# A searched order of work, smaller transfers and paired stores in an attention-and-filter kernel on one core

## The chip, the cores and the metric

The kernel runs on one core of a Trainium2 chip. The metric is the device time of one execution in microseconds (us), lower is better. "Span" is the time from the first to the last instruction in the profiled execution; it is about 1.7 us shorter than the device time of the same execution. Unless a sentence says otherwise, "clock" is the clock that was granted to TensorE, as a share of full speed.

A run is called slow when it is over 1.5% above the fastest run of the same kernel; the others are called fast. Ratios use fast runs alone.

## The reference, cut to what matters

Two branches work on the same x (2048 rows of 640, bf16) and are mixed row by row by a gate. Branch A is attention in four segments of 512 rows, 32 heads of 20, with a memory M, z that is carried from segment to segment. Branch B is a filter: a 2-D FFT, a product with complex weights, and the inverse FFT.

```python
for s in range(4):                                  # branch A, segments of 512 rows
    logits = einsum('bhqd,bhkd->bhqk', qs, ks) * scale + mask
    a_dot  = einsum('bhqk,bhkd->bhqd', softmax(logits), vs)
    pq     = phi(qs)                                # where(t > 0, t + 1, exp(t))
    a_mem  = einsum('bhld,bhde->bhle', pq, M) / (einsum('bhld,bhd->bhl', pq, z)[..., None] + 1e-6)
    outs.append(g * a_mem + (1 - g) * a_dot)        # g = sigmoid(beta), one number a head
    M = M + einsum('bhld,bhle->bhde', phi(ks), vs)
    z = z + phi(ks).sum over rows
a = concat(outs) @ wo
b = irfft2(rfft2(x) * (w_r + 1j * w_i))             # branch B
gate = sigmoid((x * gate_w).sum(-1, keepdims=True))
return gate * a + (1 - gate) * b
```

## The kernel before

The program does not write its instructions in the order in which they are to run. It first records about 2,400 operations. Each has the engines that may do it, its predecessors, an estimated duration and a priority (a time at which it would be wanted). A list scheduler inside the program then simulates the engines, gives each engine the ready operation of lowest priority, and fixes order, engine, PSUM bank and DMA semaphore. The simulation decides only the order: on the chip each engine waits for semaphores, so a wrong duration gives no wrong result, only waits.

In the simulation of the kernel before, a DMA moves 230 bytes a ns and lands 1,900 ns later, every issue takes 450 ns, and a matmul always runs at full clock.

```python
class Sched:
    HOP = 70.0
    DMABW = 230.0
    ...
                fn, occ, lat = o.alts[e]
                busy_until[e] = now + occ
                if o.dma:
                    st = max(bw_free, now + occ)
                    bw_free = st + o.nbytes / self.DMABW
                    ...
                    o.t1 = bw_free + 1900.0
```

The operations that the argument touches are these. `fold` on VectorE and GpSimd prepares x for the FFT (tiles `xf`, `xsb`), and matmuls with `fcat` transform it into `Ac`. `xt_load` brings a segment's x transposed, by a DMA that transposes. `proj_tile` computes one 128-row tile of q or k, evicts it from PSUM to one of three staging tiles `qu`, and stores it to a scratch tensor in HBM. The "pad" loads bring it back with each head's 20 rows at a partition offset of 32, and read 32 rows to do so.

```python
    O_STEP, FIN, V0, XT1 = 7.35, (4.71, 1.77), 3.96, 4.43      # XT1: priority of the second segment's xt_load
    ...
    def proj_tile(self, s, which, t, prio, xT, xb):
        ...
        self.quc = getattr(self, "quc", -1) + 1
        qi = self.quc % 3
        qu, qb = self.qu[qi], b("qu", qi)
        ...
        self.Sc.op(self.copy_alts(lambda: qu.ap(0, [1, L]), lambda: self.ps(bank, 0, [1, L]), L),
                   r=[bank], w=[qb], prio=prio, name="ev_proj")
        scr = self.qd if which == "q" else self.kd
        self.dma(lambda: dap(scr.ap(), s * 656 * L + t * P * L, [L, P], [1, L]), lambda: qu.ap(0, [1, L]),
                 P * L * 2, [qb], [b(which + "d", s, t)], prio, name="st_" + which)
    ...
    # pad loads: for each group of heads j, 32 rows of the scratch tensor to partitions 32 j ...
    dst = pad.ap(g0 * L, [L, 4 - g0], [1, L], p0=32 * j, np_=32)
    src = dap(scr.ap(), s * 656 * L + (320 * half + 80 * g0 + 20 * j) * L, [L, 32], [80 * L, 4 - g0], [1, L])
    ...
    # finish_tile: 128 rows of the output, as 4 x 32 rows
    self.dma(lambda: dap(self.out, (s * L + 4 * a) * D, [D, 4], [16 * D, 32], [1, D]), lambda: ot.ap(0, [1, D]), P * D * 2, otb,
             [b("out", s, a)], prio, name="st_out")
```

In the profile every matmul has one line (a helper), L548 before and L567 after, so matmuls are told apart by their tiles.

The softmax here doesn't subtract the row's maximum and nothing guards it: scores larger than these inputs give would overflow.

## Time and profile before

| kernel before | |
|---|---|
| median of 3 runs | 286.04 us (285.66 to 289.02) |
| profiled run: span, mean clock | 282.7 us, 0.951 |
| TensorE (PE) busy | 252.3 us, 89% |
| VectorE (DVE), ScalarE (ACT), GpSimd (POOL) busy | 201.2, 202.8, 194.6 us |
| end of the last matmul | 276.6 us |
| half-clock windows of 3.413 us before that | 7 |

The last row is from the clock record in the trace: its half-clock stretches last 13.653, 3.413, 3.413 and 3.413 us.

First some lines of the page of the kernel before. PE, DVE and PEclk are rows of 40 equal slices of 7.1 us: busy tenths of TensorE and VectorE, and the granted clock in tenths. The last line shown is the chain of work that ended last, by engine.

```profile
span 282.7 us, 8310 instructions
PE 252.3 (89%) x3356; PEld 144.4 (51%) x3376; DVE 201.2 (71%) x523; ACT 202.8 (72%) x205; POOL 194.6 (69%) x265
...
PE   8997975999889999596999998999899899999991
...
DVE  0379999598699788955899889797978454344410
...
PEclk9999985799799999888999999999999999999997
...
PE 61%; DVE 19%; ACT 5%; DMA 4%; POOL 4%; issue 4%; SPq 1%; DVEq 0%
```

TensorE is the spine. The clock row dips near 40 to 54, 77 and 120 to 136 us, which are the four stretches of the clock record (40.0 to 53.6, 74.1 to 77.5, 118.5 to 121.9 and 132.1 to 135.5 us). Stretches of 10 us show the two places that matter most. The columns are: stretch, length, busy us (and instructions) of PE, its weight loads, DVE, ACT and POOL, then the granted clock, the DMA share and GB/s.

```profile
40.00:50.00 10.00, 6.29 (x75) 3.47 (x75) 9.76 (x22) 7.05 (x7) 8.48 (x9) 0.50 0.83 186
50.00:60.00 10.00, 9.95 (x128) 5.13 (x128) 6.17 (x14) 7.40 (x8) 8.43 (x12) 0.82 0.32 74
...
110.00:120.00 10.00, 6.91 (x74) 4.16 (x73) 9.96 (x32) 7.77 (x8) 8.33 (x13) 0.92 0.75 186
120.00:130.00 10.00, 8.78 (x118) 4.15 (x117) 4.78 (x12) 7.64 (x7) 6.40 (x8) 0.91 0.54 152
130.00:140.00 10.00, 8.48 (x87) 5.10 (x89) 8.15 (x21) 6.63 (x11) 9.25 (x13) 0.83 0.49 129
```

At 40 to 50 us TensorE does 6.29 us of work at half clock while VectorE is full. Busy time at half clock counts half: in the four half-clock stretches TensorE was busy for 18.6 us, so full clock would have saved 9.3 us.

What it waits for stands in the timeline of TensorE in the kernel before (start, duration, what, and in brackets the idle time before it and what ended that):

```profile
43.78 0.61 PE L548 MATMUL psum<-qp_108,kp_110 20*128 20x256 bf16 x8 [1.66 <-ACT ex L1064]
...
49.77 1.91 PE L548 MATMUL psum<-xT_98,wq 128*128 128x512 bf16 x4 [1.07 <-DVE xsb L809]
...
119.06 1.91 PE L548 MATMUL psum<-xT_97,wk 128*128 128x512 bf16 x4 [2.47 <-ACT et_103 L936]
...
130.14 0.99 PE L548 MATMUL psum<-big,Ac 128*128 128x161 bf16 x6 [1.31 <-DVE qu_100 L558]
```

The second line is the first matmul on the second segment's x. The last one waited for VectorE to evict into the staging tile `qu_100`, and VectorE's own timeline says why that was late:

```profile
129.40 0.69 DVE L558 CAST qu_100<-psum 128x512 bf16<-128x512 f32 x1 [3.41 <-DMA k_scr<-qu_100]
```

VectorE sat idle for 3.41 us until the store of the tile's previous contents had landed. That store stood late in the DMA queue of SyncE (SPq: start of an issue and its length):

```profile
115.36 3.10 SPq L575 DMA_TRANSPOSE xT_98<-in_A_x_dram  x1
...
127.35 0.53 SPq L577 DMA_DIRECT2D k_scr<-qu_100  x1
```

The end has no holes to fill. The last pieces of the chain (start, duration, what):

```profile
224.94 34.80 PE psum L548 x542
...
262.12 14.51 PE psum L548 x353
276.65 0.44 ACT ot_87 L556
```

### The profile page before, as it was taken

How to read it: one execution, taken by the hardware profiler on the slowest of the kernel's cores; microseconds unless marked ns; L12 is line 12 of the kernel's file. 1: busy time of each engine (PE TensorE's matmuls, PEld its weight loads, DVE VectorE, ACT ScalarE, POOL GpSimd, SP SyncE). 2: the span in 40 equal slices, each digit the busy share in tenths (PEclk: the TensorE clock that was granted, in tenths of full speed). 3: DMA queues.
4: the chain of work that ended last, by engine and by line, in shares of the span. 5: the costliest groups of instructions: out<-in, count | busy, mean ns of one | idle time of the engine just before them, and what ended most of it. 6: DMA issues, size and time to landing. Idle time of an engine off the chain costs nothing.

```text
span 282.7 us, 8310 instructions
## 1 busy us (share of the span) xinstructions
PE 252.3 (89%) x3356; PEld 144.4 (51%) x3376; DVE 201.2 (71%) x523; ACT 202.8 (72%) x205; POOL 194.6 (69%) x265
## 2 busy tenths in 40 slices
PE   8997975999889999596999998999899899999991
PEld 2432543364547466244555565656465645454590
DVE  0379999598699788955899889797978454344410
ACT  1485477787784878686778897888689877667441
POOL 7059778979866757785989977898778745253410
PEclk9999985799799999888999999999999999999997
DMA  8956999254995675955624766513475403763112
GB/s 183 314 173 180 286 192 205 54 157 122 261 148 118 156 181 141 237 151 143 129 87 127 124 133 217 157 57 112 99 189 156 81 20 78 108 105 84 60 48 73
DMA packets 59270, 39.91 MB, mean 141 GB/s; under 512 B 32168, under 2 KB 55512, under 8 KB 59224
## 3 DMA queue, kind: packets, MB, share of 16 engines
q1 hardware_dynamic: 57920, 38.89, 56.9%
q10 hardware_dynamic: 1312, 0.49, 0.7%
q8 instruction: 26, 0.43, 0.6%
q14 instruction: 12, 0.10, 0.1%
HBM read 22.98 MB, written 9.97 MB: 117 GB/s over the span
## 4 chain that ended last, share of the span: by engine, by line
PE 61%; DVE 19%; ACT 5%; DMA 4%; POOL 4%; issue 4%; SPq 1%; DVEq 0%
PE psum L548 61%; ACT ex L1064 4%; DVE xsb L809 4%; DMA xT_97<-in_A_x_dram 2%; DMA gbc<-g_scr 1%; SPq L577 1%; DVE va_112 L972 1%; POOL ex L1067 1%; DVE Ac L558 1%; DVE Cp L558 1%; DVE et_102 L946 1%; POOL fbg_83 L907 1%; POOL fbg_82 L907 1%; DVE xf_118 L804 1%; DVE Pt_67 L1213 1%
## 5 line engine op out<-in xcount | busy, mean ns | idle before, releaser
L1064 ACT ACTIVATE ex<-psum 128x2048 bf16<-128x2048 f32 x80 | 150.1, 1876 | 27.2 <-PE psum L548 26.4
L1067 POOL TENSOR_SCALAR_AFFINE_SELECT ex<-ex 128x512 bf16<-128x512 bf16 x128 | 80.9, 651 | 43.2 <-ACT ex L1064 40.6
L548 PEld LDWEIGHTS psum<-va_112,ex 128*128 128x128 bf16 x640 | 19.1, 97 | 4.1 <-ACT qu_99 L556 0.8
L548 PEld LDWEIGHTS psum<-va_113,ex 128*128 128x128 bf16 x640 | 18.6, 96 | 5.0 <-issue 1.6
L548 PE MATMUL psum<-va_113,ex 128*128 128x21 bf16 x640 | 20.2, 173 | 1.0 <-POOL ex L1067 0.8
L548 PE MATMUL psum<-va_112,ex 128*128 128x21 bf16 x640 | 20.1, 174 | 0.7 <-ACT qu_99 L556 0.7
L548 PE MATMUL psum<-big,Ac 128*128 128x161 bf16 (+2 forms) x96 | 18.1, 322 | 2.1 <-DVE qu_100 L558 1.3
L548 PE MATMUL psum<-qp_108,kp_110 20*128 20x128 bf16 (+3 forms) x256 | 16.5, 312 | 2.0 <-ACT ex L1064 1.7
L548 PE MATMUL psum<-xT_97,wk 128*128 128x512 bf16 (+1 forms) x86 | 15.2, 391 | 2.7 <-ACT et_103 L936 2.5
L548 PE MATMUL psum<-big,Cp 128*128 128x321 bf16 (+1 forms) x96 | 16.7, 301 | 0.4 <-DVE G L558 0.4
L548 PE MATMUL psum<-qp_109,kp_111 20*128 20x128 bf16 (+3 forms) x256 | 16.3, 307 | 0.8 <-ACT gate_128 L970 0.6
L1106 POOL TENSOR_TENSOR on_116<-on_116,mem 128x320 bf16<-128x320 bf16 x16 | 12.6, 790 | 5.9 <-DVE on_116 L1098 3.4
L1218 POOL TENSOR_TENSOR Yt_68<-Pt_66 128x321 bf16<-128x321 bf16 x16 | 11.9, 750 | 6.6 <-DVE Pt_66 L1213 4.7
L548 PE MATMUL psum<-wv,xT_97 128*128 128x500 bf16 (+1 forms) x80 | 13.8, 307 | 2.8 <-DVE q_9_79 L558 1.5
L1213 DVE TENSOR_TENSOR Pt_67<-psum,Wt_63 128x321 bf16<-128x321 f32 x32 | 14.1, 482 | 2.5 <-PE psum L548 2.5
L548 PE MATMUL psum<-xT_97,wq 128*128 128x512 bf16 (+1 forms) x86 | 15.3, 386 | 0.6 <-DMA xT_97<-in_A_x_dram 0.4
L1213 DVE TENSOR_TENSOR Pt_66<-psum,Wt_62 128x321 bf16<-128x321 f32 x32 | 14.1, 482 | 1.9 <-PE psum L548 1.9
L548 PE MATMUL psum<-xT_98,wq 128*128 128x512 bf16 x44 | 14.0, 442 | 1.6 <-DVE xsb L809 1.1
L548 PE MATMUL psum<-wv,xT_98 128*128 128x500 bf16 (+1 forms) x80 | 14.4, 300 | 0.0
L548 PEld LDWEIGHTS psum<-big,Ac 128*128 128x128 bf16 x96 | 9.6, 113 | 7.6 <-DVE Cp L558 2.1
L1218 POOL TENSOR_TENSOR Yt_69<-Pt_67 128x321 bf16<-128x321 bf16 x16 | 11.7, 739 | 1.9 <-DVE Pt_67 L1213 1.9
L548 PE MATMUL psum<-xT_98,wk 128*128 128x512 bf16 x44 | 12.0, 381 | 0.2
(214 smaller groups left out, 546.7 us busy)
## 6 DMA issues: line engine op xcount, KB each, us to landing
xsb<-in_A_x_dram SPq DMA_DIRECT2D x8, 320.0 KB, 4.6
qp_109<-q_scr SPq DMA_DIRECT2D x16, 128.0 KB, 2.7
kp_111<-k_scr SPq DMA_DIRECT2D x16, 128.0 KB, 3.0
tt_59<-tab_tt SPq DMA_DIRECT2D x6, 256.0 KB, 2.7
qp_108<-q_scr SPq DMA_DIRECT2D x12, 128.0 KB, 4.2
kp_110<-k_scr SPq DMA_DIRECT2D x12, 128.0 KB, 2.7
tt_60<-tab_tt SPq DMA_DIRECT2D x5, 256.0 KB, 3.8
tt_61<-tab_tt SPq DMA_DIRECT2D x5, 256.0 KB, 3.2
```

What stands on the lines that cost most here:

```text
L548: h = e.matmul(o_, l_, r_, start=st, stop=sp_, **kw)
L558: alts["dve"] = (lambda e: e.tensor_copy(dst(), src()), 75 + 1.04 * n, 85.0)
L577: return e.dma_start(d_, s_)
L804: self.either(lambda e, r=r, op=op: e.tensor_tensor(xf.ap(r * 642, [321, 2], [1, 320]), xs.ap(o, [D, 2], [1, 320]), xs.ap(o + 320, [D, 2], ...
L809: self.either(lambda e, dst=dst, src=src, d0=d0, n=n, op=op: e.tensor_tensor(xs.ap(o + dst, [D, 2], [1, n]), xf.ap(src + d0, [321, 2], [1, ...
L907: fn = lambda e: e.tensor_tensor(fb.ap(0, [L, 2], [32, 16], [1, 32]), self.fcat.ap(256 + 32 * s, [P, 2], [0, 16], [1, 32]), self.gbc.ap(0, ...
L946: fmin = lambda e: e.tensor_scalar(et.ap(0, [1, L]), et.ap(0, [1, L]), 1.0, None, ALU.min)
L1064: self.one("act", lambda e: e.activation(dst(), src(), ACT.Exp, scale=SC), 4 * width, [bank], [self.exb(s, g, j) for g, j in outs], prio - ...
L1067: self.one("pool", lambda e, g=g, j=j: e.affine_select(self.ex.ap(self.exo(s, g) + JOFF[j], [1280, 4], [1, P]), self.ex.ap(self.exo(s, g) ...
L1106: add(*args, lambda e, g=g: e.tensor_tensor(on.ap(80 * g, [D, 4], [1, 80]), on.ap(80 * g, [D, 4], [1, 80]), self.mem.ap(80 * g, [D, 4], [1 ...
L1213: self.one("dve", lambda e, r=r, ri=ri, Pt=Pt, Wt=Wt, bank=bank: e.tensor_tensor(Pt.ap((2 * r + ri) * 322, [1, KD]), self.ps(bank, 0, [1, ...
L1218: fn = lambda e, r=r, a0=a0, a1=a1, op=op, Pt=Pt, Yt=Yt: e.tensor_tensor(Yt.ap(r * 322, [1, KD]), Pt.ap(a0 * 322, [1, KD]), Pt.ap(a1 * 322 ...
```

## The change

The intent is to let a search choose the order. The search ran ahead of time against an improved simulation, and its result is a table of 1,353 offsets that are added to the priorities. The simulation now has figures for how long a transfer takes to issue and its rows to move, and it assumes that the clock falls when a window of 3,413 ns is not busy enough. Beside that, q and k tiles are stored in pairs, the pad loads read 20 rows in place of 32, two scratch loads that fed the surplus rows are gone, the second segment's transposed x is asked for earlier (`XT1`), and some small operations for the memory's mask and epsilon are cheaper. With the pairs the room for staged q and k tiles grows from three tiles to four (two buffers of two tiles).

```diff
+    def schedule(self, pools, plan=(), nsem=56):
+        for o in ops if plan else ():
+            o.prio += plan[o.key] / 10.0
...
+                if e == "pe":
+                    occ *= self.pe_slow(now, occ)
...
-                    bw_free = st + o.nbytes / self.DMABW
+                    bw_free = st + o.xfer
-                    o.t1 = bw_free + 1900.0
+                    o.t1 = bw_free + 2000.0
...
+    def pe_slow(self, now, occ):
+        w = int(now / 3413.0)
+        while self.win < w:
+            busy = self.winbusy.get(self.win, 0.0) / 3413.0
+            self.slow = 2.0 if busy < (0.65 if self.slow == 1.0 else 0.85) else 1.0
+            self.win += 1
...
-        return self.Sc.op({queue: (f, 450.0 if queue == "sp" else 80.0, 0.0)}, ...
+        cost = 700.0 + nbytes / 260.0 if tr else 580.0 if nbytes in (41088, 163840) else 430.0
+        row = 256.0 if tr else self.ROWS.get(name, 1024.0)
+        xfer = nbytes / row * (9.0 + row / 26.3) / 16 * 1.15
+        return self.Sc.op({queue: (f, cost, 0.0)}, ..., xfer=xfer)
...
-    O_STEP, FIN, V0, XT1 = 7.35, (4.71, 1.77), 3.96, 4.43
+    O_STEP, FIN, V0, XT1 = 7.35, (4.71, 1.77), 3.96, 1.5
+    PLAN = (-238, -224, 123, 67, ... 1,353 numbers in all ...)
-                self.Sc.schedule({"qk": [0, 1, 2, 3], "gen": [4, 5, 6, 7]})
+                self.Sc.schedule({"qk": [0, 1, 2, 3], "gen": [4, 5, 6, 7]}, self.PLAN)
-        self.qu = [T(f"qu{i}", [P, L]) for i in range(3)]
+        self.qu = [T(f"qu{i}", [P, 2 * L]) for i in range(2)]
...
-                        return pad.ap(g0 * L, [L, 4 - g0], [1, L], p0=32 * j, np_=32)
+                        return pad.ap(g0 * L, [L, 4 - g0], [1, L], p0=32 * j, np_=DH)          # DH = 20
...
-        self.dma(lambda: dap(scr.ap(), s * 656 * L + t * P * L, [L, P], [1, L]), lambda: qu.ap(0, [1, L]),
-                 P * L * 2, [qb], [b(which + "d", s, t)], prio, name="st_" + which)
+        if t in (1, 2, 4):
+            n, o = len(both), qo - slot * L
+            self.dma(lambda: dap(scr.ap(), s * 640 * L + (t - slot) * P * L, [L, P], [P * L, n], [1, L]),
+                     lambda: qt.ap(o, [L, n], [1, L]),
+                     n * P * L * 2, both, [b(which + "d", s, pair)], prio, name="st_" + which)
```

(Cuts are marked with "..."; the groups that give each operation its key, and the small operations of the memory, are left out.)

## The prediction

> **What bounds it now.** TensorE: the page gives 252.3 us busy of 282.7, and 61% of the chain that ended last is matmul; no other engine passes 72%. From 225 to 276.7 us the matmul stream has almost no gap and only a store follows; that end cannot shrink unless work leaves it. Before it about 24 us of TensorE time is idle, 1.7 us of that the start, the rest holes at 34-52, 68-76, 82-92, 112-119 and 126-133 us (table of short stretches).
>
> The holes cost twice. The Trainium skill ("TensorE: Matmul & The Clock Gate", Part 1) says the clock falls to half after an idle window of about 3.4 us. This trace agrees: in slices of 3.41 us the granted clock is 0.50 from 41 to 51 us, and 0.65 near 75, 120 and 133 us, each after slices with less matmul (1.64, 2.7, 0.81, 1.82 us). Busy time within the half-rate parts is some 18 us, so full clock would save up to 9 us (estimate). Holes plus clock: about 31 us at most.
>
> Why holes: at 19-50 us VectorE is the chain (9.8-10.0 us busy in every 10): folds, evictions, small pieces. TensorE has little else: the second segment's transposed x is issued only at 36.4 us (5.3 us of issue), its first matmul runs at 49.8. At 125-129 us VectorE idles 3.4 us for a q/k buffer whose k store was issued late, behind a queue that was issuing for 28.5 of the 30 us from 100 to 130 us (transposes 1.2-5.3 us each, 64 weight loads of 0.6 us).
>
> **What the change does.** The compiled orders have the same 3376 matmuls, VectorE 523 to 522 instructions, GpSimd 265 to 256. DMA issues go from 272 to 254 (two scratch loads gone, 40 q/k stores become 24): at about 0.4 us, 7 us less of 186 us of queue time (estimate). Pad loads carry 20 of 32 rows, 2.9 MB less of 39.9. Some evictions move between VectorE and ScalarE, with little net shift early. The real change is order: the second segment's x is issued ahead of the k loads, and its q, v and k matmuls stand between the fold transforms, in the 34-52 us hole. A paired store delays its first tile by one projection (about 1.2 us).
>
> **On the critical path.** Hole and clock at 34-60 us: worth 5-6 us. Holes at 112-136 us with their clock: 3-4. Elsewhere 1-2. Removed DMA work helps only through these. Some comes back: the same 128x512 VectorE operation takes 0.28 to 0.7 us and more here, which a plan with fixed durations cannot place exactly, so new holes will open. Net about 10 us.
>
> **Predicted: 276 us, 80% range 267-284.** Faster by over 2%: 0.72; within 2%: 0.22; slower: 0.06.
>
> **Right or wrong in the profile.** Span near 273; matmul busy about 246, from clock alone; mean granted clock 0.97 or more; no 0.50 stretch at 41-51; first second-segment matmul near 35 instead of 50; queue time down about 7 us; a gapless end of about 50 us still there; the last matmul 5-6 us before the end.
>
> **What would break it.** Early x delays the first segment's k loads, so ScalarE's exponentials start late and pile up; VectorE stays full until 50 us whatever TensorE does; buffers of pairs come free later; the clock's windows fall elsewhere than the plan's.

## The result, and the profile after

| | before | after |
|---|---|---|
| median of 4 runs | 287.53 us (285.66 to 289.75) | 272.64 us (272.45 to 273.02) |
| profiled run: span, mean clock | 282.7 us, 0.951 | 270.9 us, 0.985 |
| PE busy | 252.3 us | 244.7 us |
| end of the last matmul | 276.6 us | 262.5 us |
| half-clock windows before that | 7 | 1 |
| DMA moved | 39.91 MB | 36.83 MB |

The ratio is 0.9481, with a 95% interval of 0.9397 to 0.9565. A ratio is the mean time of one kernel's fast runs over that of the other's in the same rounds, so it is not quite the ratio of the medians in the table. The change is faster by about 5%.

The same lines of the page of the kernel after:

```profile
span 270.9 us, 8271 instructions
PE 244.7 (90%) x3354; PEld 145.4 (54%) x3376; DVE 204.1 (75%) x522; ACT 203.3 (75%) x207; POOL 192.4 (71%) x256
...
PE   8998698679999999998989999999999999999970
...
DVE  0179999979999989998999999889986653444300
...
PEclk9999979999999999999999999999999999999996
...
PE 59%; DVE 24%; ACT 5%; POOL 4%; DMA 4%; issue 2%; DVEq 0%; SPq 0%
```

One stretch at half clock is left, within the work, where there were four. From these numbers the gain splits into three terms. PE busy time fell by 7.6 us (252.3 to 244.7) for the same 3376 matmuls. Idle time of TensorE before its last matmul fell from 24.3 to 17.8 us (276.6 − 252.3 and 262.5 − 244.7), which is 6.5. The end after the last matmul grew from 6.1 to 8.4 us, which is −2.3. Together that is 11.8 us, the difference of the two spans.

The fall of busy time is the clock and nothing else: matmul time at half clock went from 18.6 to 3.4 us, and half of that difference is 7.6 us.

The same stretches of 10 us, kernel after:

```profile
40.00:50.00 10.00, 8.34 (x105) 4.70 (x103) 9.93 (x26) 5.79 (x10) 6.33 (x8) 1.00 0.43 131
50.00:60.00 10.00, 6.49 (x79) 3.55 (x77) 9.58 (x21) 8.78 (x10) 8.05 (x11) 1.00 0.49 124
...
110.00:120.00 10.00, 9.38 (x111) 4.81 (x112) 9.80 (x30) 8.55 (x9) 9.53 (x13) 1.00 0.94 191
120.00:130.00 10.00, 9.01 (x106) 5.39 (x110) 8.93 (x21) 8.87 (x10) 9.54 (x14) 1.00 0.55 139
130.00:140.00 10.00, 9.44 (x147) 6.05 (x144) 9.83 (x23) 8.20 (x8) 9.99 (x14) 1.00 0.42 107
```

TensorE is not fuller at 50 to 60 us (6.49 us of 10), but what it does there runs at full clock. At 110 to 140 us it has 27.8 us of work where it had 24.2, and VectorE no longer falls to 4.78 of 10.

Because the two kernels order work differently, clock times do not compare directly. A fairer measure is how much matmul work was done by when, with busy time at half clock counted half. Both programs have the same matmuls, so equal work is an equal distance along the program, though not the same instructions:

| full-clock matmul work done (us) | reached before | reached after | lead of after |
|---|---|---|---|
| 30 | 33.6 | 37.1 | −3.5 |
| 40 | 54.2 | 49.0 | 5.2 |
| 50 | 64.2 | 62.7 | 1.5 |
| 80 | 99.5 | 94.1 | 5.4 |
| 110 | 138.2 | 126.2 | 12.0 |
| 200 | 233.5 | 219.3 | 14.2 |

So the stretch up to 94 us gained 5.4 us and the stretch up to 126 us another 6.6. The rest up to the last matmul gained 2.1 (276.6 − 262.5 is 14.1), and the end gave 2.3 back.

The timeline of TensorE in the kernel after shows one of the holes that are left early on, and the first matmul on the second segment's x, now at 40.15 us:

```profile
34.09 1.96 PE L567 MATMUL psum<-wv,xT_88 128*128 128x141 bf16 x8 [1.23 <-DVE va_102 L1055]
...
40.15 2.10 PE L567 MATMUL psum<-xT_89,wq 128*128 128x512 bf16 x9
```

The queue of SyncE has the k stores at 122.9 us, with 8 issues between the transposing load and them, where there were 13:

```profile
112.27 5.00 SPq L594 DMA_TRANSPOSE xT_89<-in_A_x_dram  x1
...
122.91 0.40 SPq L596 DMA_DIRECT2D k_scr<-qu_90  x1
```

The last pieces of the chain after, in answer to the three shown of before:

```profile
203.04 43.63 PE psum L567 x740
246.70 1.89 ACT ex L1149
248.64 1.14 POOL ex L1152
249.83 12.68 PE psum L567 x315
262.52 0.44 ACT ot_77 L575
```

### The profile page after: what moved, and what is told of

Read it like the earlier page. It is cut to its first block, busy times and chain, and to the rows that moved or that the text cites. A ratio compares the mean times of both kernels' runs of the same rounds, so it can differ in the third digit from the quotient of the medians.

```text
span 270.9 us, 8271 instructions
## 1 busy us (share of the span) xinstructions
PE 244.7 (90%) x3354; PEld 145.4 (54%) x3376; DVE 204.1 (75%) x522; ACT 203.3 (75%) x207; POOL 192.4 (71%) x256
## 2 busy tenths in 40 slices
DMA packets 55735, 36.83 MB, mean 136 GB/s; under 512 B 31521, under 2 KB 51985, under 8 KB 55697
## 4 chain that ended last, share of the span: by engine, by line
PE 59%; DVE 24%; ACT 5%; POOL 4%; DMA 4%; issue 2%; DVEq 0%; SPq 0%
PE psum L567 59%; DVE xsb L877 4%; ACT ex L1149 3%; DMA gbc<-g_scr 2%; DVE phq L1029 2%; DVE qu_90 L577 2%; DVE et_93 L1028 1%; DVE et_92 L1028 1%; DMA k_scr<-qu_90 1%; DVE phk_95 L1029 1%; DVE xf_110 L872 1%; POOL fbg_72 L980 1%; DVE va_102 L1055 1%; POOL fbg_73 L980 1%; DVE Pt_67 L1302 1%
## 5 line engine op out<-in xcount | busy, mean ns | idle before, releaser
L567 PEld LDWEIGHTS psum<-va_102,ex 128*128 128x128 bf16 x640 | 18.1, 96 | 4.1 <-POOL ex L1152 1.2
L567 PEld LDWEIGHTS psum<-va_103,ex 128*128 128x128 bf16 x640 | 18.3, 96 | 3.5 <-issue 0.8
L567 PE MATMUL psum<-va_103,ex 128*128 128x21 bf16 x640 | 19.1, 172 | 0.7 <-DVE Cp L577 0.5
L567 PE MATMUL psum<-va_102,ex 128*128 128x21 bf16 x640 | 19.2, 173 | 0.6 <-POOL ex L1152 0.5
L567 PE MATMUL psum<-big,Ac 128*128 128x161 bf16 (+2 forms) x96 | 17.8, 318 | 0.7 <-DVE Pt_67 L1302 0.5
L567 PE MATMUL psum<-qp_98,kp_100 20*128 20x512 bf16 (+3 forms) x256 | 15.8, 301 | 1.9 <-ACT ex L1149 1.2
L567 PE MATMUL psum<-wv,xT_88 128*128 128x500 bf16 (+1 forms) x80 | 14.8, 328 | 2.8 <-DVE va_102 L1055 2.7
L567 PE MATMUL psum<-qp_99,kp_101 20*128 20x512 bf16 (+3 forms) x256 | 15.9, 301 | 0.2
L567 PE MATMUL psum<-wv,xT_89 128*128 128x500 bf16 (+1 forms) x80 | 14.3, 301 | 0.6 <-DVE Ac L577 0.6
L1302 DVE TENSOR_TENSOR Pt_66<-psum,Wt_62 128x321 bf16<-128x321 f32 x32 | 14.1, 481 | 0.7 <-PE psum L567 0.6
L577 DVE CAST G<-psum 128x321 bf16<-128x321 f32 x24 | 11.2, 490 | 4.4 <-PE psum L567 4.3
L567 PE MATMUL psum<-xT_88,wq 128*128 128x512 bf16 (+1 forms) x85 | 14.0, 380 | 0.4 <-issue 0.3
L567 PE MATMUL psum<-xT_89,wq 128*128 128x512 bf16 x44 | 11.7, 381 | 0.9 <-DVE mem L1092 0.6
L1192 POOL TENSOR_TENSOR on_106<-on_106,mem 128x320 bf16<-128x320 bf16 x15 | 11.8, 795 | 0.8 <-DVE on_106 L1184 0.8
L1030 POOL TENSOR_TENSOR phq<-phq,et_93 128x512 bf16<-128x512 bf16 x9 | 10.6, 1172 | 2.5 <-DVE et_93 L1028 2.5
```

Of the source, the lines that this page charges most:

```text
L567: h = e.matmul(o_, l_, r_, start=st, stop=sp_, **kw)
L577: alts["dve"] = (lambda e: e.tensor_copy(dst(), src()), 75 + 1.04 * n, 85.0)
L1030: fadd = lambda e: e.tensor_tensor(dst(), dst(), et.ap(0, [1, L]), ALU.add)
L1192: add(*args, lambda e, g=g: e.tensor_tensor(on.ap(80 * g, [D, 4], [1, 80]), on.ap(80 * g, [D, 4], [1, 80]), self.mem.ap(80 * g, [D, 4], [1 ...
L1302: self.one("dve", lambda e, r=r, ri=ri, Pt=Pt, Wt=Wt, bank=bank: e.tensor_tensor(Pt.ap((2 * r + ri) * 322, [1, KD]), self.ps(bank, 0, [1, ...
```

## The experiments

Three causes were held against each other: the new order (by the plan); the new transfers (pairs of stores, 20-row pads); and the planner's new figures, with the early transpose, whatever the offsets. Some of the quoted texts name theories by letters; in the first call A is the order and B the transfers. Twelve kernels ran on three chips. Kernels of one chip shared 11 runs of the kernel before: median 288.34 us on the first chip, 287.89 on the second, 287.69 on the third. All outputs were correct.

On the second and third chips only 4 and 5 of the 11 runs of the kernel before are fast, and the record's verdict on every kernel run there is "unclear", the kernel after included. The intervals are given all the same; a difference of 1 or 2% there is weak. On the first chip the verdicts are slower (x1_no_plan), faster (x2_old_transfers, x6_last_stores) and same (x8_no_clock_model).

Half-clock windows below are counted in a profiled run of each kernel, up to its last matmul.

### x1_no_plan: everything but the offsets

```diff
-                self.Sc.schedule({"qk": [0, 1, 2, 3], "gen": [4, 5, 6, 7]}, self.PLAN)
+                self.Sc.schedule({"qk": [0, 1, 2, 3], "gen": [4, 5, 6, 7]})
```

> The changed kernel with the 1,100 searched offsets left out; its new cost figures, smaller pad loads and paired stores stay. Theory A (the searched order is what saves): most of the 14 us is lost again, 281 to 287 us, with new holes and half-clock stretches in the first 140 us. Rival B (fewer and smaller transfers save) and rival C (better cost figures alone save): 272 to 276 us.

Measured: 299.35 us (297.69 to 299.99, 4 runs), ratio to before 1.0376 (1.0318 to 1.0434).

The other parts of the change, without the offsets, are slower than the kernel before: the transfers, the early transpose and the planner's figures do not carry the gain. The theory of order stands, but its number (near the kernel before) was missed on the slow side. Why it is slower than the kernel before was not tried by itself; the likely reason, argued from x12_ten_ns below, is that the old priorities suit the old figures of the planner. On its own base the plan is worth about 27 us (299.35 against 272.64, on two chips).

### x2_old_transfers: the order of after, with the old transfers

Each paired store is issued as two stores in its place, and the pad loads read 32 rows again (except where a row would fall outside). Order, engines and banks are those of the kernel after.

```diff
-            self.dma(lambda: dap(scr.ap(), s * 640 * L + (t - slot) * P * L, [L, P], [P * L, n], [1, L]), lambda: qt.ap(o, [L, n], [1, L]),
+            self.dma(lambda: [dap(scr.ap(), s * 656 * L + (t - slot + x) * P * L, [L, P], [1, L]) for x in range(n)],
+                     lambda: [qt.ap(o + x * L, [1, L]) for x in range(n)],
...
-                        return pad.ap(g0 * L, [L, 4 - g0], [1, L], p0=32 * j, np_=DH)
+                        return pad.ap(g0 * L, [L, 4 - g0], [1, L], p0=32 * j, np_=DH if half and j == 3 else 32)
```

> The changed kernel, every engine in exactly its order, but each paired store issued as two stores and the pad loads carrying 32 rows again (all but the one that would read past the end). Theory A: the transfers matter only through waits, so 273 to 274.5 us, at most 2 us above the changed kernel's 272.6. Rival B: 278 us or more, with the DMA queue as the new waiter.

Measured: 279.9 us (277.03 to 282.32, 6 runs); its three fast runs have a mean of 277.63, the ratio to before is 0.9631 (0.9573 to 0.969). The kernel after was not run on this chip. Beside x6_last_stores of the same rounds, told below, which differs from it only in the last stores, the old transfers cost 3.5 us by the means of the fast runs (277.63 and 274.18) and 4.8 by the medians (279.9 and 275.08); beside the kernel after on the other two chips (272.64 and 272.82) it is about 5 of fast runs. That is more than the theory of order allowed (274.5). That of the transfers asked for 278 or more: the fast runs stay just below, the median of all six is above. The execution that was profiled first was a slow one (280.1 us); the trace that is kept is of a fast one (277.5 us). Two lines of SyncE's queue in the fast one:

```profile
116.71 3.48 SPq L597 DMA_TRANSPOSE xT<-in_A_x_dram  x1
...
125.79 1.34 SPq L595 DMA_DIRECT2D k_scr<-qu  x3
```

The transposing load starts at 116.71 us, 4.4 us later than after, and the k stores behind it at 125.79 instead of 122.91. VectorE waits 0.59 us for one of them, and the clock does not fall there; it falls at 33, 57 and 200 us, three half-clock windows where the kernel after had one. The idle time of TensorE before its last matmul is 22.2 us instead of 17.8. In the slow execution the k stores came at 127.22 us, TensorE waited at about 130 us for an eviction into a staging tile, as before, and the clock fell from 129.7 to 137 us. So the late stores are in both, but the fall at 130 us is only in the slow one.

### x9_pads_32 and x10_two_stores: each transfer undone alone

These are the two halves of x2_old_transfers: x9_pads_32 has only the 32-row pads, x10_two_stores only the split stores.

> The changed kernel in its own order, only the pad loads with 32 rows again (no store split). With both undone the kernel took 277 to 282 us, with the q/k stores issued 4.3 us later near 125 us and a new hole with half clock after it; pad loads there took 0.46 us of issue and more against 0.36. If the pads are the larger part (64 issues, 0.1 us each and more): 274.5 to 278 us. If the stores are: 272 to 273.5 us.

> The changed kernel in its own order, only the paired stores issued as two again (16 more issues of about 0.4 us). If stores are the larger part: 275 to 278 us. If pads are: 272 to 274 us, queue time up by about 7 us all the same.

Measured: 278.28 us (276.95 to 280.14, 4 runs), ratio 0.9742 (0.9641 to 0.9842), for the pads; 277.4 us (276.6 to 278.51, 4 runs), ratio 0.9729 (0.9651 to 0.9807), for the stores. All eight runs are fast ones. The kernel after itself was not run on this chip, but x11_last_two, told below, is that kernel with other last stores, and its fast runs there have a mean of 271.15 us, an estimated 1.5 less than the kernel after would take. So each half alone costs about 5 us (4.8 for the stores, 5.8 for the pads), and both together cost about the same (277.63 in the fast runs of x2_old_transfers, on another chip): the costs do not add.

In its profile x10_two_stores does the same work as the kernel after at the same time, to about 1.5 us, until 198 us. Then it loses its time in one stretch (from 205.3 to 212 us):

```profile
205.30:212.00 6.70, 6.70 (x73) 3.38 (x70) 3.03 (x9) 4.60 (x4) 6.07 (x7) 0.51 0.20 60
```

TensorE is busy throughout and at half clock throughout: two windows of 3.413 us, so 3.4 us lost. The profile of x9_pads_32 has four half-clock windows, near 34, 58, 130 and 202 us, where the kernel after had one. The reading that fits all three is that a small delay in a queue widens a hole that was just too small for the clock to fall, and which hole that is depends on the delay. It is a reading and not shown: the kernel after itself falls at other holes in other runs (after_again, below).

### x3_early_x: the kernel before with only the early transpose

```diff
-    O_STEP, FIN, V0, XT1 = 7.35, (4.71, 1.77), 3.96, 4.43
+    O_STEP, FIN, V0, XT1 = 7.35, (4.71, 1.77), 3.96, 1.5
```

> The kernel before with one number changed: the second segment's transposed x is asked for at 1.5 instead of 4.43 in the plan's own time, so its issue stands before the first k loads and its matmuls between the fold transforms, as in the changed kernel. Theory A (TensorE had nothing to do at 34-52 us because x came late): the hole and its half-clock stretch go, 3 to 5 us saved, ratio 0.983 to 0.990. Rival D (VectorE is full until 50 us either way, and the k loads come later): no gain, ratio 0.995 to 1.01.

Measured: 289.63 us (287.89 to 291.46, 4 runs), ratio 1.0192 (1.0076 to 1.0308). The same two stretches as above:

```profile
40.00:50.00 10.00, 6.69 (x72) 3.44 (x68) 9.14 (x17) 8.91 (x11) 8.90 (x10) 1.00 0.71 180
50.00:60.00 10.00, 8.44 (x117) 5.53 (x117) 9.50 (x21) 6.45 (x8) 8.82 (x13) 0.66 0.25 53
```

The early transpose does lift the clock at 40 to 50 us, and 40 us of matmul work are done at 44.4 us instead of 54.2. But it only moves the trouble: VectorE is now nearly full until 60 us, TensorE waits for its evictions, the clock falls at 50 to 57 us, and 60 us of work are reached at 76.0 us against 77.3, 80 us at 99.0 against 99.5. Nearly the whole lead is given back. The ratio is even above what rival D expected, but it rests on four fast runs of the kernel before; by the medians it is 1.006. Either way nothing is saved. The prediction named the early transpose as the cure of the first hole; that it is so by itself is refuted.

### x4_four_buffers: the kernel before with a fourth staging tile

The order, engines, banks and semaphores of the kernel before are kept exactly: the program is recorded a second time with four `qu` tiles in place of three, and takes its order from the first. To make room, a mask is kept in bf16.

```diff
-        qi = self.quc % 3
+        qi = self.quc % self.NQ          # 3 while the order is made, then 4
...
-        self.hmf = T("hmf", [P, 880], F32)
+        self.hmf = T("hmf", [P, 880])
```

> The kernel before in exactly its order on every engine, but with four staging buffers for q and k tiles instead of three (room from keeping a mask in 16 bits; the result may differ in the last digits). If the hole at 126-133 us comes from an eviction that waits for the buffer of a k store issued late: it goes, with its half-clock stretch, 2.5 to 4 us saved, ratio 0.986 to 0.991. Rival: the next wait takes its place, ratio 0.996 or more.

Measured: 282.51 us (280.06 to 285.41, 4 runs) beside 287.89 for before; ratio of the fast runs 0.9856 (0.9743 to 0.997), about as expected (two of its four runs are fast). The wait of VectorE for the k store is gone, and so is the fall of the clock at 133 us:

```profile
120.00:130.00 10.00, 9.56 (x114) 5.19 (x114) 6.99 (x16) 8.91 (x9) 8.99 (x12) 0.94 0.60 158
130.00:140.00 10.00, 8.50 (x101) 4.87 (x99) 9.40 (x26) 7.89 (x11) 8.40 (x13) 1.00 0.55 150
```

Its profile has five half-clock windows (four at 39 to 53 us, one at 118 us) against seven: the one at 74 us is gone too. There ScalarE evicts the same tile, first in the kernel before, then in this one:

```profile
70.51 0.60 ACT L556 ACTIVATE qu_99<-psum 128x512 bf16<-128x512 f32 x1 [1.17 <-PE psum L548]
...
68.69 0.60 ACT L556 ACTIVATE qu<-psum 128x512 bf16<-128x512 f32 x1
```

The profile puts the first wait down to TensorE, but its matmuls for this tile had ended at 68.46 us; the k store from `qu_99` had been issued at 67.33 us, which points to a wait for that store. With a fourth tile the eviction follows its matmuls within 0.1 us. By the matmul work done, the lead over the kernel before is 2.0 us when 60 us are done, and 4.6 when 110 are. So waits for a staging tile in two places were worth about 4 us, some 2.6 of it at 126 to 136 us, in an order that is otherwise that of the kernel before. This is direct support for what the prediction said of 125 to 136 us.

### x8_no_clock_model and x12_ten_ns: the plan under another planner

The first keeps the offsets but takes the falling clock out of the simulation. The second changes one planner figure that has nothing to do with the clock, the delay after which a finished operation releases another, from 70 to 80 ns.

```diff
-                    occ *= self.pe_slow(now, occ)        # x8_no_clock_model
+                    pass
...
-    HOP = 70.0                                           # x12_ten_ns
+    HOP = 80.0
```

> The changed kernel, offsets kept, but the planner's clock model off (matmuls always at full rate in the plan). If offsets and model are one fitted thing: 275 to 283 us, as the order falls apart (491 rows of the matmul order differ). If knowledge of the clock hardly matters: 271 to 274 us.

> The changed kernel, offsets and clock model kept, with one unimportant figure of the planner changed: 80 instead of 70 ns for a semaphore's way. 459 rows of the matmul order differ, about as many as with the clock model off (491, 290 us). If offsets fit only the very model they were searched with: 280 to 291 us, and the run without the clock model says nothing about the clock. If order is robust and the clock model mattered: 272 to 277 us.

Measured: 290.26 us (289.56 to 292.12, 4 runs), ratio 1.0089 (1.0023 to 1.0156), without the clock model, which is worse than either expectation; 289.98 us (287.93 to 292.65, 4 runs), ratio 1.0143 (1.0044 to 1.0243), with 10 ns more. The clock row of x12_ten_ns, from a slow run:

```profile
PEclk9999999689997596899997999999959999999996
```

Taking out the clock model loses the whole gain, which alone would look like proof that the clock model is the gain. It is not: changing an unrelated figure by 10 ns loses it as well, because it makes 459 places of TensorE's order differ. As far as these two changes show, the offsets fit only the very simulation that they were searched with. What share of the gain the clock model brought stays open; to learn it, the search would have to be repeated without it.

### x5_filler: dummy matmuls to hold the clock

To price the clock alone, two dummy matmuls of 128x512 were put before each of the last twelve fold transforms in the order of before, where its clock falls.

```diff
+            fill = e == "pe" and o.name == "F1" and o.first and self.FILL[0] <= nf < self.FILL[1]
...
+        for k in range(2):
+            self.nc.tensor.matmul(self.ps(o.banks[0], 0, [1, L]), w.ap(k * P, [1, P]), w.ap(0, [1, L]), start=True, stop=True)
```

> The kernel before in exactly its order, with two dummy 128x512 matmuls ahead of each of the last twelve fold transforms, into the bank they overwrite: they keep TensorE busy while it waits at 36-70 us. The granted clock should stay 1.0 at 41-53 us. If the half clock there cost time, as my prediction counted: 3 to 5 us saved, ratio 0.983 to 0.990. If VectorE is the chain there, clock is worth little: ratio 0.996 to 1.006.

Measured: 290.24 us (287.22 to 292.34, 4 runs), ratio 1.0179 (1.0054 to 1.0304). In the profiled run (a slow one) the clock fell all the same from 39 to 49 us. The dummies came with the transforms and did not fill the holes between them, so the experiment did not make what it was to measure, and nothing is concluded from it.

### after_again: the kernel after once more

> The changed kernel once more, on this chip, as the reference for the runs that alter it: 271 to 276 us. If it has the two levels that the run with split last stores showed (272 and 275 us), these come from where the clock's windows fall; its profile should then differ from the first one in one half-clock stretch of 3.4 us.

Measured: 272.82 us (272.48 to 277.32, 6 runs), ratio 0.9616 (0.9538 to 0.9695). The result stands on a second chip, with a gain of 3.8% by the fast runs. Its profiled run (275.64 us, fast) shows the clock row

```profile
PEclk9999999979999999999999999999899999999995
```

with dips at 56 to 60 us and 196 to 200 us, and none at 34 to 38 us where the first profile has its only one. It is the same program. The Trainium skill ("TensorE: Matmul & The Clock Gate", Part 1, "What's actually happening") says that the window of 3413 ns is free-running and does not start with the kernel. These traces agree as far as they can: each half-clock stretch before the last matmul lasts a whole number of 3.413 us (3.413, 6.827, 10.240 or 13.653), and runs of one program fall at different holes. So the times come in levels: its six spans on this chip are 270.7 to 271.2, 273.9 and 275.6 us.

The same shows in the kernel before. Over its 11 runs on this chip, the time at half clock (2 × (1 − mean clock) × span) goes from 24.8 to 40 us, and the span follows it with a correlation of 0.92 and a slope of 0.5 us per us, which is what the half rate alone would cost. On the first and the third chip the same fit gives a correlation of 0.80 and 0.91 and a slope of 0.34 and 0.40, so the figure is rough. The kernel after spends 6.5 to 14.3 us at half clock in its runs, which includes a few us at the end, when TensorE has finished.

### x6_last_stores and x11_last_two: the end

Measured ends: the last eviction to the end of the span took 5.6 us before (277.09 to 282.7) and 7.9 us after (262.96 to 270.9). The queue of SyncE shows what differs. Kernel before:

```profile
275.21 0.54 SPq L577 DMA_DIRECT2D out_dram<-ot_86  x1
277.12 0.54 SPq L577 DMA_DIRECT2D out_dram<-ot_87  x1
```

Kernel after:

```profile
260.95 0.54 SPq L596 DMA_DIRECT2D out_dram<-ot_76  x1
261.63 0.54 SPq L596 DMA_DIRECT2D out_dram<-ot_75  x1
262.99 0.54 SPq L596 DMA_DIRECT2D out_dram<-ot_77  x1
```

And two stretches of 2 us of the kernel after, when only these stores run (the DMA share and the GB/s are the last two columns):

```profile
264.00:266.00 2.00, 0.00 (x0) 0.00 (x0) 0.00 (x0) 0.00 (x0) 0.00 (x0) 1.00 0.25 92
266.00:268.00 2.00, 0.00 (x0) 0.00 (x0) 0.00 (x0) 0.00 (x0) 0.00 (x0) 0.58 0.27 100
```

A share of 0.25 is that of four of the 16 DMA engines. The Trainium skill ("DMA: Bandwidth & Descriptors", "Why a DMA increments its semaphore by 16 and not by 1") says that a transfer gets the largest number of engines, up to 16, that divides the slowest dimension of both sides. The output is written as 4 x 32 rows, so its slowest dimension is 4, and the trace agrees with that rule. A store of 163,840 bytes at about 92 GB/s takes an estimated 1.8 us. Before, the last stores were issued 1.9 us apart; after, they come 0.7 and 1.4 us apart. The search packed the last tiles more closely, and its simulation does not know that these stores use four engines. They queue up in both kernels, though: the DMA records of the two traces show the last four stores moving without a break, from 273.5 to 281.7 us before and from 260.5 to 268.4 us after. From the last eviction to the last packet it is 4.6 us before and 5.4 after.

That is only 0.8 of the 2.3 us by which the end grew. The other 1.5 us come after the last packet: 1.0 us to the end of the span before, 2.5 after. The program ends with a loop on SyncE that waits for its 56 DMA semaphores one after the other (`for s_, c in zip(dsem, dcnt): ... nc.sync.wait_ge(s_, c)`). The simulation had given the last store a semaphore with 6 more behind it before and 24 after, and from one wait to the next it is 0.06 us. So this is a cost of the order in which the semaphores are waited for; none of the expectations saw it, and no run changed it.

x6_last_stores splits each of the last four stores into four of 32 rows, all from SyncE:

```diff
+        if s == 3:
+            dst = lambda: [dap(self.out, (s * L + 4 * a + q) * D, [16 * D, 32], [1, D]) for q in range(4)]
+            src = lambda: [ot.ap(0, [1, D], p0=32 * q, np_=32) for q in range(4)]
```

> The changed kernel in its own order, but the four stores of the last segment each issued as four of 32 rows. After its last matmul 8.5 us pass (6.1 before the change), with the DMA engines at a share of 0.25 to 0.27: the stores' slowest dimension is 4, and the Trainium skill's DMA page says that sets how many of the 16 engines are used. If so, the end shrinks by 2.5 to 4 us: 268.5 to 270.3 us, share in the last slices well over 0.3. Rival: the end is write latency whatever the shape: 272 us or more (longer by the 12 more issues).

Measured: 275.08 us (271.6 to 275.61, 6 runs), ratio 0.9512 (0.9453 to 0.9571). In a trace of it the end after the last eviction took 7.0 us instead of 7.9. The 16 issues took 7.31 us, so the transfers, now wide, came no faster than they were issued. The expected 2.5 to 4 us were missed: the gain was under 1 us and is lost in the levels of the clock, for of its six runs two took 272 us and four 275. The loop over the semaphores still took its 2.5 us after the last packet.

x11_last_two splits only two stores, those of tiles 0 and 2 of the last segment, and issues half of the latter from ScalarE's queue:

```diff
+        for qs, queue in (((0, 1, 2, 3), "sp"),) if s == 3 and a == 0 else (((0, 1), "sp"), ((2, 3), "act")) if s == 3 and a == 2 else ():
+            self.dma(lambda qs=qs: [dap(self.out, (s * L + 4 * a + q) * D, [16 * D, 32], [1, D]) for q in qs],
+                     lambda qs=qs: [ot.ap(0, [1, D], p0=32 * q, np_=32) for q in qs], P * D * 2, otb,
+                     [b("out", s, a, queue)], prio, name="st_out", queue=queue)
```

> The changed kernel in its own order; of the four last stores only the two that end last are cut into four of 32 rows, and half of the very last goes to ScalarE's queue. With all four cut on one queue the end was bound by 16 issues of 0.46 us: 7.0 us after the last eviction instead of 7.9. Here the last issue should end about 265 us instead of 267: an end of 4.5 to 6 us, 269.5 to 271.5 us in executions without an extra half-clock stretch. If the end is write latency: 272 us.

Measured: 271.33 us (270.25 to 275.09, 6 runs), ratio 0.9507 (0.9444 to 0.9571). In its profiled run the end took 6.3 us, and the transfers ran at twice the share:

```profile
268.00:270.00 2.00, 0.00 (x0) 0.00 (x0) 0.00 (x0) 0.00 (x0) 0.00 (x0) 0.99 0.65 188
```

That is 1.6 us less than the 7.9 of the kernel after, where 4.5 to 6 in all had been expected: 3.2 us to the last packet instead of 5.4, and then 3.0 us for the loop over the semaphores. Its median is the lowest of all that ran, but it was not run in the same rounds as the kernel after, whose medians were 272.64 and 272.82 us on other chips. Only the shorter end in its trace is shown.

## Why the prediction was right or wrong

The prediction was 276.0 us (267 to 284), faster with 0.72. Measured were 272.64 us. The point was 3.4 us too high, within the range.

- **What bounds the kernel.** "The holes cost twice" was right and is the main lesson. The two costs were 6.5 us of idle time and 7.6 us of half clock, before 2.3 were given back at the end. The net was foreseen as about 10 and measured as 11.8 in the profiles.
- **The first hole: size right, cause wrong.** "Hole and clock at 34-60 us: worth 5-6 us." Measured was a lead of 5.4 us, though only by 94 us, with 1.5 at 63. That the size agrees is luck as far as the stated reason goes. This reason, that the second segment's x comes earlier and fills the hole, failed as a cause of its own: x3_early_x does that and nothing else, and takes 289.63 us. The first matmul on that x came at 40.15 us, not "near 35". What the runs show in its place is the order as a whole. What in the early order does it was not taken apart further. One part is visible: the exponentials of the first segment start later (the seventh at 50.0 us instead of 38.6, the 20th still at 86.5 instead of 80.9), and VectorE is nearly full until 60 us, where before it was so until 50. The prediction listed this as what would break it ("VectorE stays full until 50 us whatever TensorE does"). It happened, and did not break it: in this run the holes that it left made the clock fall only once.
- **The holes at 112 to 136 us: mechanism right, size too small.** "Holes at 112-136 us with their clock: 3-4." Measured was 6.6 us between the points where 80 and 110 us of matmul work are done. x4_four_buffers shows the mechanism: with one staging tile more and nothing else of the order changed, the wait and the fall of the clock at 133 us vanish and about 2.6 us with them. The kernel after has room for four tiles too, by its pairs. How much of this stretch is owed to that room and how much to the order, no run here separates.
- **Transfers.** "Removed DMA work helps only through these" was right in kind: x9_pads_32 and x10_two_stores cost some 5 us each, through holes and clock windows. But the sentence reads as if it were little, and about a third of the gain is lost if either is missing. "Queue time down about 7 us" was short. Summed over the single issue records of the two traces, it went from 177.1 to 166.1 us: stores of q and k with their scratch loads −8.2, pad loads −6.3, transposing loads +2.7, the rest +0.7. The pads' term was not in the sum: a load of 20 rows takes a median of 0.34 us to issue, one of 32 rows 0.43, and there are 64. (The spans of merged lines in the timeline hold the gaps between issues and show far less.)
- **The end: wrong.** "The last matmul 5-6 us before the end" and "that end cannot shrink" took the end as fixed. It grew to 8.4 us: 0.8 us because the last stores queue up longer on four DMA engines, and 1.5 us because more semaphore waits stand behind that of the last store. The gapless end itself was still there: from 203.0 to 262.5 us TensorE is idle for 0.2 us in all.
- **New holes.** "New holes will open" was right, and which they are differs from run to run.
- **The clock.** Mean clock 0.985 where 0.97 or more was said, no half clock at 41 to 51 us, busy time 244.7 where 246 was said. The prediction quoted the Trainium skill ("TensorE: Matmul & The Clock Gate", Part 1), by which the clock falls after an idle window of about 3.4 us, and took the trace to agree. The length and the half rate agree with every fall in the traces read here. "Idle" does not: the windows of the clock record ahead of the falls were 74, 68, 40 and 43% busy before and 21% after (busy by the profile, whose matmul ends are modelled; the prediction's slices did not lie on these windows). The same page, under "A second HAM failure mode: psum-queue depth-cycling", tells of frequent short idle times that make the clock swing, without a threshold; that is nearer to what is seen here.

What is open: how much of the gain the search would have found without a model of the clock; what in the early order, beside the transpose, makes the first hole harmless; and what exactly decides a window. Windows of 57, 69, 71, 73 and 75% busy also passed without a fall before, windows of 54, 66, 66 and 77% after. One of 45% passed in x10_two_stores, and one of 45% made the clock fall in after_again. So the busy share alone, with the planner's thresholds of 0.65 and 0.85, is only an approximation.

## What to carry to other kernels

A hole on the engine that bounds the kernel may cost twice, once as idle time and once as half clock afterwards; so count half-clock windows in several runs before explaining a difference of a few us, since one program can fall at different holes. A plan that was searched against a simulation belongs to that simulation: after any change of a figure or a transfer, search again, and do not read the loss from removing one part of the model as the worth of that part. After tightening the order, look at the end: these stores, whose outer dimension is 4, kept a quarter of the DMA engines busy, and the waits that close the program can stand in an order that makes the last one late.

## What the Trainium skill lacked or had wrong

- "TensorE: Matmul & The Clock Gate", Part 1: the fall of the clock is put down to an idle window. Here it fell after windows of 3.413 us in which TensorE was 74, 68, 43, 40 and 21% busy (by the profile), and did not fall after others of 54 to 77%, nor after one of 45% in x10_two_stores. The page gives no busy share, and the runs do not settle one.
- The same page: the way back is given as at least one busy window, without saying how busy or when one is not enough. Here the clock stayed at half after windows of 62 to 66% busy (40 to 50 us in the kernel before), and in x10_two_stores it stayed at half for two windows (6.8 us) in which TensorE was busy all the time.
- The same page treats what the free-running window changes from run to run only at the start of a kernel, and as a small matter. Here one program's times differ by 3.5% (282.46 to 292.3 us in 11 runs on one chip), and they follow the time at half clock (0.5 us per us there, 0.34 and 0.40 on the two other chips).
- "DMA: Bandwidth & Descriptors" has no issue time of a strided load by its number of rows: here a median of 0.34 us for 20 rows and 0.43 us for 32 rows, both of four 1 KB pieces a row, and 0.54 us for an output store of 128 rows of 1,280 bytes.
- "DMA: Bandwidth & Descriptors", "Rules for kernel authors", advises to use all 16 engines and says that another queue only saves issue time. Both agree with x6_last_stores and x11_last_two; what the section lacks is that splitting a store for width can leave it bound by issue (16 issues took 7.31 us, at a DMA share of 0.31 to 0.36).
